# Attention's weight pieces in one transfer each instead of four, v stored from GpSimd's queue, and later loads of w_o and of attention's output

## The chip, the core and the metric

The kernel runs on one NeuronCore of a Trainium2 chip. Its five engines work at the same time and wait for each other through semaphores: TensorE (PE, with its weight loads as PEld), VectorE (DVE), ScalarE (ACT), GpSimd (POOL) and SyncE (SP), which here only issues DMA transfers. Sixteen DMA engines move data between the chip's memory (HBM) and the on-chip memory (SBUF, 128 partitions). The metric is device time in microseconds (us).

## The reference

One layer for x of 2048 rows by 448, in float32: attention with 16 heads of 28 columns, and a gated feed-forward network of width 1792, mixed row by row with a sigmoid gate.

```python
def _A_ref(x, wqkv, wo):
    qkv = transpose((x @ wqkv).reshape(B, S, 3, H, Dh), 2, 0, 3, 1, 4)
    q, k, v = qkv[0], qkv[1], qkv[2]
    scores = einsum("bhqd,bhkd->bhqk", q, k) * (Dh ** -0.5)
    p = softmax(scores, axis=-1)
    o = einsum("bhqk,bhkd->bhqd", p, v)
    return transpose(o, 0, 2, 1, 3).reshape(B, S, D) @ wo

def _B_ref(x, w_gate, w_up, w_down):
    return (gelu(x @ w_gate) * (x @ w_up)) @ w_down

g = sigmoid((x * gate_w).sum(-1, keepdims=True))
return g * _A_ref(x, wqkv, wo) + (1 - g) * _B_ref(x, w_gate, w_up, w_down)
```

## The kernel before

A float32 product is made of three products of rounded parts (high times high, high times low, low times high), so most operands exist as a high and a low half, which `parts` makes with a copy and a subtraction.

The program has four stages, one after the other on PE.

1. **q and k** (to about 82 us). `qk_tile` makes 28 tiles of q and k, which SP stores to `qkd`. On the side, x is loaded a second time in another layout (`xraw`, `load_x32`, 32 rows for each of four groups of partitions) and split by DVE into `X32`. Four groups of 32 partitions let four small matrix products run at the same time on PE, one for each quarter of the rows of x.
2. **v** (to about 116 us). `v_tile` makes 16 tiles of v. After every fourth, a group of four (928 KB) is stored to `vd`, from ACT's queue. Two buffers `V` are used in turn, so ACT may write the third group only when the store of the first has landed. At the same time `prepare(b)` splits a block of w_up or w_gate on GpSimd and stores it to `wsd` in an order of its own: per block two half-steps of 32 rows. `load_piece(m)` reads one piece of it back, into a tile `w0` (1024 columns) or `w1` (768 columns), once into each of the four groups of partitions, because each group needs the same weights for its own quarter of x. Each tile has three buffers.
3. **Attention** (about 117 to 819 us). PE interleaves three kinds of products: the scores of a head (`b<-Q,K`), the feed-forward network's x @ w_up and x @ w_gate (`b<-X,w`, called crosses), and after each half head the weights times v (`b<-pt,VH`). The order of all of it is made before the kernel runs by `plan`, which counts time with fixed costs: each of the four groups walks through its crosses in steps (`pos[r]`, starting at `OFFSET` and ending at `goal[r]`), 21 steps to two pieces, and a `load` stands where the group that is furthest back has left an old piece behind. ACT takes the exponentials, DVE copies finished crosses to `u`, SP stores them to `ud`. `finish` and `divide` send the row sums of a head through memory (`dend`, `r`, `rdend`, `rb`) on GpSimd's queue, and store the head's output to `od`.
4. **Down** (about 835 us to the end). The last block's crosses (`PG`, the last four pieces, 112 to 115) stand at its beginning, from 819 us. Then 56 units (`UNITS`, four blocks of 512 rows times `NF` = 14) each load `hu` and `hg` from `ud`, apply gelu, multiply, split into `hl`, and PE multiplies by w_down (`b<-W,hl`, 12 products to a unit). `load_wo` loads and splits w_o, `load_o` a quarter of attention's output, `project` multiplies them, and `gather` scales the results by the gate and adds them.

What sets the order of the DMA transfers: SP's queue is issued strictly in the program's order, and one transfer that waits holds up all behind it. Besides waits on data, each transfer on SP and ACT counts on one of eight semaphores that are used in turn, and waits until the transfer before it on the same semaphore has landed; GpSimd's queue has eight of its own.

Of the kernel before, what the change touches and what calls it, by code (L numbers as in the profile page):

```python
# [7 lines left out]
F32 = mybir.dt.float32  # L8
# [8 lines left out]
S, D, H, DH, F = 2048, 448, 16, 28, 1792  # L17
P = 128
# [5 lines left out]
NF = F // P  # L24
# [20 lines left out]
NEVER = 1 << 60  # L45
# [6 lines left out]
def piece(n):  # L52

    return n // 21 * 2 + (n % 21 >= 12)


def plan(blocks):
# [5 lines left out]
    goal = [21 * blocks + o for o in OFFSET]  # L63
    pos = list(OFFSET)
# [9 lines left out]
    def take():  # L74
        b = bank.index(min(bank))
        bank[b] = NEVER
        return b
# [23 lines left out]
    def run_dve(ready):  # L101
        nonlocal dve
        dve = max(dve, ready) + COPY
        return dve + BACK
# [17 lines left out]
    def can_cross(r):  # L122
        return pos[r] < goal[r] and piece(pos[r]) < parted

    def step():
        nonlocal now, parted, loaded
        did = []
        for r in range(4):
            if score[r]:
                key, b, n = score[r]  # L130
                ops.append(("score", r, key, n, b))
                score[r][2] += 1
                did.append((r, True))
            elif can_cross(r) and (mine[r] or min(bank) <= now):
                first = mine[r] is None
                mine[r] = ["cross", r, pos[r], take() if first else mine[r][3], first, False]
                ops.append(mine[r])
                pos[r] += 1
                did.append((r, False))
        now += STEP  # L140
        for r, s in did:
            if s and score[r][2] == 3:
                end_score(r)
            if not s and (pos[r] % 42 == 0 or pos[r] == goal[r]):
                mine[r][-1] = True
                b, mine[r] = mine[r][3], None
                bank[b] = run_dve(now + SEEN)
                ops.append(("clear", r, pos[r] - 1, b))
        while loaded < 2 * blocks + 8 and piece(min(pos)) >= loaded - 5:
            ops.append(("load", loaded))  # L150
            loaded += 1
            arrive.append(now + LOAD)
        while arrive and arrive[0] <= now:
            arrive.pop(0)
            parted += 1
# [59 lines left out]
def gated_mix(ctx: ExitStack, tc: tile.TileContext, xT, wqk, wvg, wg, wu, wd, wo, sel, ident, out):  # L215
    nc = tc.nc

    pin = tc.keep_in_program_order

    def mm(o, lhsT, rhs, start, stop):  # L220
        return pin(nc.tensor.matmul(o, lhsT, rhs, start=start, stop=stop))  # L221

    def by_sp(out, in_):
        return pin(nc.sync.dma_start(out=out, in_=in_))  # L224

    def by_pool(out, in_):
        return pin(nc.gpsimd.dma_start(out=out, in_=in_))  # L227
# [5 lines left out]
    def act_copy(o, i):  # L233
        return nc.scalar.activation(o, i, AF.Copy)  # L234
# [6 lines left out]
    vd = dram.tile([P, 4, H, 4, VC], F32, name="vd")  # L241
    wsd = dram.tile([2 * NF, 2, 32, 14, P], F32, name="wsd")
    shd = dram.tile([H, 2, S], F32, name="shd")
    od = dram.tile([D, S], F32, name="od")
    dend = dram.tile([H, S], F32, name="dend")
    rdend = dram.tile([H, S], F32, name="rdend")
# [9 lines left out]
    def group(r):  # L256
        return slice(32 * r, 32 * r + 32)
# [6 lines left out]
    def load_x32():  # L264
        c, k, n = UNITS[len(xraw)]
        j, b = (c, k) if k < 4 else (2 + c, k - 4)
        raw = st.tile([P, 2, TB], F32, name="xraw", bufs=2)
        for r in range(4):
            by_sp(raw[group(r), 0:n], xT[r, 32 * j:32 * j + 32, b:b + n])
        xraw.append(raw)  # L270

    def split_x32(u):
# [22 lines left out]
    def load_piece(m):  # L295
        c, a = divmod(m, 2)
        b = c // 2 if c < WRAP else len(BLOCKS) - 1 if c >= WRAP + 2 else 0
        w = halves[m] = fw.tile([P, 2, 4 - a, P], F32R, name=f"w{a}", bufs=3)
        for r in range(4):
            by_sp(w[group(r)].bitcast(F32), wsd[b, c % 2, :, 8 * a:8 + 6 * a].rearrange("p (a n) m -> p a n m", a=2))  # L300

    def step_of(n):

# [21 lines left out]
        parts(Qt[h % 2][:, 0], Qt[h % 2][:, 1], qraw, pool_copy, pool_sub)  # L325

    def load_shift(h, dma):
        for r in range(4):
            half = slice(r // 2 * 1024, (r // 2 + 1) * 1024)
            dma(Qt[h % 2][32 * r + DH:32 * r + DH + 2, 0].bitcast(F32), shd[h, :, half])  # L330

    with ExitStack() as ph:
        xp = ph.enter_context(tc.tile_pool(name="xp", bufs=1, side="right"))
# [135 lines left out]
        Qt = [p.tile([P, 2, S // 2], F32R, name=f"Q{j}") for j, p in enumerate((kt, kq))]  # L469
# [8 lines left out]
        def v_tile(i):  # L478
            V = VS[i // 4 % 2]
            p = psv.tile([P, VW], F32, name="pv")  # L480
            for j, (x, w) in enumerate(PAIRS):
                m = mm(p, X[:, x, i * P:(i + 1) * P], WV[:, w, :], j == 0, j == len(PAIRS) - 1)
            a = pin(act_copy(V[:, :, i % 4, 0:DH], p[:, 0:D].rearrange("p (h d) -> p h d", h=H)))
            pin(act_copy(gate[:, 0, i:i + 1], p[:, D:D + 1]))
            if i % 4 == 3:
                pin(nc.scalar.dma_start(out=vd[:, i // 4], in_=V))
            return m, a

        prepare(0)
# [7 lines left out]
        for m in range(2):  # L497
            load_piece(m)
# [35 lines left out]
    with tc.If(bounded < 1, label="rows"):  # L534
        with ExitStack() as ph:
# [5 lines left out]
            for h in range(H):  # L541
                Q = gp.tile([DH, 2, S], F32R, name="gQ")
                K = gp.tile([DH, 2, S], F32R, name="gK")
                for first, dst in ((h * DH, Q), (D + h * DH, K)):
                    raw = gp.tile([DH, S], F32, name="graw")
# [3 lines left out]
                m = gp.tile([P, NT], F32, name="gm")  # L549
                for i in range(NT):  # L550
                    p = gps.tile([P, S], F32, name="gsc")
                    for c in range(S // 512):
                        for n, (a, b) in enumerate(((0, 0), (1, 0), (0, 1))):
# [11 lines left out]
                                  in_=ms.bitcast(F32))  # L565
# [7 lines left out]
    ends, sums = [], {}  # L573

    def finish(h, o):
        for j in range(4):
            by_pool(dend[h:h + 1, j * 512:(j + 1) * 512], o[j * 32 + DH:j * 32 + DH + 1])
        r = op.tile([P, S // P], F32, name="r")
        by_pool(r, dend[h].rearrange("(p n) -> p n", p=P))
        ends.append((h, o, r))  # L580

    def divide():
        while ends:
            h, o, r = ends.pop()
            pin(nc.vector.reciprocal(r, r))
            by_pool(rdend[h].rearrange("(p n) -> p n", p=P), r)
            rb = op.tile([P, 512], F32, name="rb", bufs=1)
            for j in range(4):
                by_pool(rb[j * 32:(j + 1) * 32], rdend[h:h + 1, j * 512:(j + 1) * 512].to_broadcast([32, 512]))
            pin(nc.gpsimd.tensor_tensor(o, o, rb, OP.mult))  # L590
            for j in range(4):
                by_pool(od[h * DH:(h + 1) * DH, j * 512:(j + 1) * 512], o[j * 32:j * 32 + DH])
# [171 lines left out]
    def gather(tb, p, g, i):  # L764

        t = tb * 4 + i
        w = gate[:, g, t:t + 1]
        if t in Y:
            y = Y.pop(t)
            pin(nc.vector.scalar_tensor_tensor(y, p[:, 0:D], w, y, OP.mult, OP.add))  # L770
            outs.append((out[0, t * P:(t + 1) * P], y))
        else:
            y = Y[t] = yp.tile([P, D], F32, name="y", bufs=8)
            pin(nc.vector.tensor_scalar(y, p[:, 0:D], w, None, OP.mult))
# [14 lines left out]
    def load_o(tb):  # L789
        s = slice(tb * TB, (tb + 1) * TB)  # L790
        o = wl.tile([P, 4, TB], F32, name="oraw", bufs=2)
        by_pool(o[:, 0:3], od[0:3 * P, s].rearrange("(b p) n -> p b n", p=P))
        for a in (0, 64):
            by_pool(o[a:a + 64, 3], od[3 * P:, s])
        O = OHL[tb] = wl.tile([P, 7, TB], F32R, name="ohl", bufs=2)
        hr = wl.tile([P, TB], F32R, name="ohr")
        parts(O[:, 0:3], O[:, 4:7], o[:, 0:3], pool_copy, pool_sub)
        pin(pool_copy(O[0:64, 3], o[0:64, 3]))
        parts(hr[64:], O[64:, 3], o[64:, 3], pool_copy, pool_sub)

    pd, OHL = [None] * 4, {}
    for n in range(4):
        load_unit(n)
    for n in range(3):
# [7 lines left out]
    for k in range(42):  # L812
        w, a, i, j = step_of(42 * len(BLOCKS) + k)
# [9 lines left out]
    for n, (tb, f) in enumerate(UNITS):  # L823
        while outs:
            by_sp(*outs.pop(0))
        if n + EARLY < NF:
            split_f(n + EARLY)
        if n + 4 < len(UNITS):
            load_unit(n + 4)
        if n + 3 < len(UNITS):  # L830
            multiply(n + 3)
        if n + 2 < len(UNITS):
            split_unit(n + 2)
        if n in (2, 4, 6, 8):
            last_gate(n // 2 - 1)
        if n == 2:
            divide()
        if n == 3:
            load_wo()
        if n in (8, 20, 30, 44):  # L840
            load_o((8, 20, 30, 44).index(n))
        if f == 0 and tb > 1:
            for a in range(tb - 2 if tb == 2 else 1, tb):
                if a < tb - 1 or tb == 3:
                    project(a)
        down(n)
        if f == NF - 1:
            for i in range(4):
                gather(tb, pd[i], 2, i)
    project(NTB - 1)  # L850
    while outs:
        by_sp(*outs.pop(0))
# [37 lines left out]
```

## Time and profile before

| | us |
|---|---|
| three runs | 1020.56, 1024.32, 1024.58 (median 1024.32) |
| the profiled execution | 1018.83 |
| its span, from the first instruction to the last | 1017.0 |
| PE busy in the span | 994.0 (98%) |
| ACT, DVE, POOL busy | 647.3, 564.1, 481.1 |
| DMA | 194.87 MB, mean 192 GB/s |

The profile shows one execution. "Busy" is the time in which an engine has an instruction; for PE the ends of pipelined products are modelled. A row of the view by stretches (`A:B`) gives for each engine the busy time and the number of instructions, then the granted clock of PE, the mean busy share of the 16 DMA engines and the GB/s that they moved. A timeline row gives the start, the time, the engine, the line, the operation and in brackets the idle time before it with what ended it. `x4` is the number of instructions that a row merges. SPq and ACTq are the DMA-issuing sequencers of SP and ACT. In the list of DMA queues, q1 is SP's.

### The profile page before, as it was taken

How to read it: one execution, taken by the hardware profiler on the slowest of the kernel's cores; microseconds unless marked ns; L12 is line 12 of the kernel's file. 1: busy time of each engine (PE TensorE's matmuls, PEld its weight loads, DVE VectorE, ACT ScalarE, POOL GpSimd, SP SyncE). 2: the span in 40 equal slices, each digit the busy share in tenths (PEclk: the TensorE clock that was granted, in tenths of full speed). 3: DMA queues.
4: the chain of work that ended last, by engine and by line, in shares of the span. 5: the costliest groups of instructions: out<-in, count | busy, mean ns of one | idle time of the engine just before them, and what ended most of it. 6: DMA issues, size and time to landing. Idle time of an engine off the chain costs nothing.

```text
span 1017.0 us, 27987 instructions
## 1 busy us (share of the span) xinstructions
PE 994.0 (98%) x11191; PEld 754.8 (74%) x11191; DVE 564.1 (55%) x851; ACT 647.3 (64%) x1238; POOL 481.1 (47%) x697
## 2 busy tenths in 40 slices
PE   9999799989999999999999999999999999999998
PEld 7888666757766777667767667776777668899997
DVE  4552055646655676546646456664666547776552
ACT  4332176868786788867878768887787845443230
POOL 5325251735566465653556657474554204534110
PEclk9999989999999999999999999999999999999999
DMA  6866665556666666655576566665657679868350
GB/s 228 252 207 209 209 211 171 172 155 174 190 187 172 182 183 189 199 158 172 156 207 195 151 201 183 196 194 163 176 176 226 190 236 305 254 200 282 112 203 36
DMA packets 109671, 194.87 MB, mean 192 GB/s; under 512 B 32736, under 2 KB 47200, under 8 KB 109536
## 3 DMA queue, kind: packets, MB, share of 16 engines
q1 hardware_dynamic: 92272, 162.12, 51.9%
q0 software_dynamic: 15856, 26.32, 9.3%
q10 hardware_dynamic: 1408, 4.59, 1.2%
q8 instruction: 90, 1.47, 0.6%
q14 instruction: 45, 0.37, 0.1%
HBM read 131.99 MB, written 60.95 MB: 190 GB/s over the span
## 4 chain that ended last, share of the span: by engine, by line
PE 79%; DMA 5%; DVE 2%; SPq 1%; issue 0%; ACT 0%; ACTq 0%; DVEq 0%
PE b L221 79%; DMA w<-wsd 3%; DMA draw<-in_wd 1%; DMA hg<-ud 1%; SPq L224 1%; DVE hu L746 1%; DVE hl L231 0%; DVE W L231 0%; ACT hg L734 0%; DMA Q<-shd 0%; DVE u L635 0%; DVE u L633 0%; DVE o L651 0%; DVE y L770 0%; ACT W L234 0%
## 5 line engine op out<-in xcount | busy, mean ns | idle before, releaser
L221 PE MATMUL b<-X,w 32*128 32x512 f32 x4704 | 480.0, 394 | 12.5 <-DMA w<-wsd 12.2
L221 PE MATMUL b<-Q,K 32*128 32x512 f32 x3072 | 445.3, 397 | 1.8 <-DMA Q<-shd 1.7
L221 PEld LDWEIGHTS b<-X,w 32*128 32x128 f32 x4704 | 413.9, 185 | 38.5 <-issue 14.8
L618 ACT ACTIVATE pt<-b 128x512 f32<-128x512 f32 x559 | 310.1, 604 | 163.6 <-PE b L221 158.2
L221 PEld LDWEIGHTS b<-Q,K 32*128 32x128 f32 x3072 | 356.2, 183 | 34.7 <-issue 19.9
L622 DVE COPY pt<-b 128x512 f32<-128x512 f32 x465 | 312.7, 689 | 72.6 <-PE b L221 52.2
L618 ACT ACTIVATE pt<-pt 128x512 f32<-128x512 f32 x465 | 268.3, 632 | 0.1
L221 PE MATMUL b<-pt,VH 128*32 128x512 f32 x2048 | 228.1, 597 | 0.0
L221 PEld LDWEIGHTS b<-pt,VH 128*32 128x32 f32 x2048 | 63.8, 110 | 146.4 <-issue 139.2
L221 PE MATMUL b<-W,hl 128*128 128x448 f32 x672 | 139.5, 369 | 3.0 <-DVE hl L231 3.0
L221 PEld LDWEIGHTS b<-W,hl 128*128 128x128 f32 x672 | 127.1, 190 | 15.0 <-DVE hl L231 4.2
L635 DVE COPY u<-b 128x512 f32<-128x512 f32 x108 | 73.0, 684 | 34.1 <-PE b L221 33.4
L221 PE MATMUL pqk<-X,WQK 128*128 128x512 f32 x308 | 74.2, 403 | 0.3 <-ACT X L234 0.3
L734 ACT ACTIVATE hg<-hg 128x512 f32<-128x512 f32 x52 | 32.6, 626 | 65.2 <-DMA hg<-ud 64.6
L653 DVE TENSOR_TENSOR o<-b,o 128x512 f32<-128x512 f32 x16 | 11.1, 692 | 113.4 <-PE b L221 113.4
L221 PEld LDWEIGHTS pqk<-X,WQK 128*128 128x128 f32 x308 | 59.3, 193 | 15.5 <-ACT X L234 1.0
L651 DVE COPY o<-b 128x512 f32<-128x512 f32 x16 | 11.1, 691 | 106.6 <-PE b L221 86.4
L227 POOL DMA_DIRECT2D wsd<-whl x112 | 59.2, 535 | 11.0 <-POOL whl L231 8.2
L746 DVE TENSOR_TENSOR hu<-hg,hu 128x512 f32<-128x512 f32 x52 | 45.2, 869 | 30.1 <-ACT hg L734 29.9
L227 POOL DMA_DIRECT2D dend<-o x64 | 31.1, 492 | 49.9 <-DVE o L653 43.1
L227 POOL DMA_DIRECT2D rb<-rdend x64 | 31.6, 501 | 44.1 <-DMA rdend<-r 44.1
L234 ACT ACTIVATE hl<-hu 128x512 fp32r<-128x512 f32 x56 | 34.9, 623 | 25.7 <-DVE hu L746 20.9
(81 smaller groups left out, 696.5 us busy)
## 6 DMA issues: line engine op xcount, KB each, us to landing
w<-wsd SPq DMA_DIRECT2D x232, 128.0 KB
ud<-u SPq DMA_DIRECT2D x111, 256.0 KB
w<-wsd SPq DMA_DIRECT2D x232, 96.0 KB
hu<-ud SPq DMA_DIRECT2D x56, 256.0 KB
hg<-ud SPq DMA_DIRECT2D x52, 256.0 KB
qkd<-q SPq DMA_DIRECT2D x28, 256.0 KB
qraw<-qkd SPq DMA_DIRECT2D x64, 112.0 KB
kraw<-qkd SPq DMA_DIRECT2D x128, 56.0 KB
```

Source lines behind the costliest of these rows:

```text
L221: return pin(nc.tensor.matmul(o, lhsT, rhs, start=start, stop=stop))
L224: return pin(nc.sync.dma_start(out=out, in_=in_))
L227: return pin(nc.gpsimd.dma_start(out=out, in_=in_))
L234: return nc.scalar.activation(o, i, AF.Copy)
L618: pin(nc.scalar.activation(PT[key], PT[key] if b is None else sc[b], AF.Exp, scale=SCALE))
L622: pin(nc.vector.tensor_copy(PT[key], sc[b]))
L635: pin(nc.vector.tensor_copy(u, ps[b]))
L651: pin(nc.vector.tensor_copy(sums["o"], po))
L653: pin(nc.vector.tensor_tensor(sums["o"], po, sums["o"], OP.add))
L734: pin(nc.scalar.activation(o, i, AF.Gelu_apprx_tanh))
L746: pin(nc.vector.tensor_tensor(u, g, u, OP.mult))
```

## The change

Attention's weight pieces, the second copy of x (`xraw`), the shift of the scores (`Q<-shd`), the row sums (`dend`) and their inverses (`rb`) each come in one or two transfers instead of four: the four copies of a piece are written as one pattern whose reading side starts with four repeats (step 0) of 32 rows, and whose writing side is 128 partitions. A group of v is stored from GpSimd's queue instead of ACT's. The planner, when it looks for the group that is furthest back, leaves out groups that have reached their goal. w_o is loaded in unit 14 instead of 3, attention's first two quarters in units 17 and 24 instead of 8 and 20, and the four `gather`s after unit 13 are spread over units 13 to 16.

```diff
@@ plan @@
-        while loaded < 2 * blocks + 8 and piece(min(pos)) >= loaded - 5:
+        while loaded < 2 * blocks + 8 and piece(min(pos[r] if pos[r] < goal[r] else NEVER for r in range(4))) >= loaded - 5:
             ops.append(("load", loaded))
@@ load_x32 @@
         raw = st.tile([P, 2, TB], F32, name="xraw", bufs=2)
-        for r in range(4):
-            by_sp(raw[group(r), 0:n], xT[r, 32 * j:32 * j + 32, b:b + n])
+        by_sp(raw[:, 0:n], xT[:, 32 * j:32 * j + 32, b:b + n])
@@ load_piece @@
-        for r in range(4):
-            by_sp(w[group(r)].bitcast(F32), wsd[b, c % 2, :, 8 * a:8 + 6 * a].rearrange("p (a n) m -> p a n m", a=2))
+        src = wsd[b, c % 2, :, 8 * a:8 + 6 * a].rearrange("p n m -> p (n m)")
+        by_sp(w.bitcast(F32).rearrange("p a n m -> p (a n m)"),
+              src.unsqueeze(0).to_broadcast([4, 32, (8 - 2 * a) * P]))
@@ load_shift @@
-        for r in range(4):
-            half = slice(r // 2 * 1024, (r // 2 + 1) * 1024)
-            dma(Qt[h % 2][32 * r + DH:32 * r + DH + 2, 0].bitcast(F32), shd[h, :, half])
+        for a in range(2):
+            dma(Qt[h % 2][DH + a::32, 0].bitcast(F32),
+                shd[h, a].rearrange("(i n) -> i n", i=2).unsqueeze(1).to_broadcast([2, 2, S // 2]))
@@ v_tile @@
             if i % 4 == 3:
-                pin(nc.scalar.dma_start(out=vd[:, i // 4], in_=V))
+                by_pool(vd[:, i // 4], V)
@@ finish @@
-        for j in range(4):
-            by_pool(dend[h:h + 1, j * 512:(j + 1) * 512], o[j * 32 + DH:j * 32 + DH + 1])
+        by_pool(dend[h].rearrange("(j n) -> j n", j=4), o[DH::32])
@@ divide @@
-            for j in range(4):
-                by_pool(rb[j * 32:(j + 1) * 32], rdend[h:h + 1, j * 512:(j + 1) * 512].to_broadcast([32, 512]))
+            by_pool(rb, rdend[h].rearrange("(j n) -> j n", j=4).unsqueeze(1).to_broadcast([4, 32, 512]))
@@ the loop over units @@
-    pd, OHL = [None] * 4, {}
+    pd, due, OHL = [None] * 4, [], {}
-        if n == 3:
+        if n == NF:
             load_wo()
-        if n in (8, 20, 30, 44):
-            load_o((8, 20, 30, 44).index(n))
+        if n in (17, 24, 30, 44):
+            load_o((17, 24, 30, 44).index(n))
         if f == NF - 1:
-            for i in range(4):
-                gather(tb, pd[i], 2, i)
+            due = [(tb, pd[i], 2, i) for i in range(4)]
+        for _ in range(1 if NF - 1 <= n < NF + 3 else len(due)):
+            gather(*due.pop(0))
```

PE's order of instructions is the same, product by product. SP's order changes at three kinds of places.

First, on SP during the v tiles, the first six pieces (names with a number are buffers; `32x1024 x4` are four transfers of 32 rows of 1024 numbers, `128x1x1024` one transfer of 128). Before:

```order
L224 DMA wraw<-in_wu 128x512
L224 DMA w_833<-wsd 32x1024 x4
L224 DMA w_838<-wsd 32x768 x4
L224 DMA w_901<-wsd 32x1024 x4
L224 DMA w_906<-wsd 32x768 x4
L224 DMA kraw<-qkd 28x2x256 x4
```

and now:

```order
L224 DMA wraw<-in_wu 128x512
L224 DMA w_809<-wsd 128x1x1024
L224 DMA w_811<-wsd 128x1x768
L224 DMA w_871<-wsd 128x1x1024
L224 DMA w_873<-wsd 128x1x768
L224 DMA kraw<-qkd 28x2x256 x4
```

The sixteen transfers ahead of `kraw` are four, with the same bytes; the same holds for every later piece.

Second, on GpSimd at the same time, where `prepare(1)`, the split of k and `prepare(2)` follow each other. Before there is no `vd` on this queue. Now (from the split of the first k to the branch after the v tiles):

```order
L230 CAST K_704<-kraw 128x256
L231 TENSOR_TENSOR K_704<-kraw,K_704 128x256
L230 CAST K_705<-kraw 128x256
L231 TENSOR_TENSOR K_705<-kraw,K_705 128x256
L227 DMA vd<-V_714 128x1856
L230 CAST whl<-wraw 128x512
L231 TENSOR_TENSOR whl<-wraw,whl 128x512
```

The first group's store stands behind the first split. A little later on the same queue, from the end of the second split:

```order
L231 TENSOR_TENSOR K_707<-kraw,K_707 128x256
L230 CAST whl<-wraw 128x512
L231 TENSOR_TENSOR whl<-wraw,whl 128x512
L227 DMA wsd<-whl 32x1024
L227 DMA wsd<-whl 32x2x384
L227 DMA wsd<-whl 32x1024
L227 DMA wsd<-whl 32x2x384
L227 DMA vd<-V_715 128x1856
L227 DMA vd<-V_714 128x1856
L227 DMA vd<-V_715 128x1856
L533 TENSOR_LOAD flag
```

The second group's store stands behind the second split of k and all of `prepare(2)`; before, it was issued by ACT right after its last copy.

Third, on SP at the end of attention, the last pieces. Before:

```order
L224 DMA ud<-u 128x512
L224 DMA hu<-ud 128x512
L224 DMA hg<-ud 128x512
L224 DMA hu<-ud 128x512
L224 DMA hg<-ud 128x512
L224 DMA ud<-u 128x512 x2
L224 DMA w_19190<-wsd 32x1024 x4
L224 DMA w_19195<-wsd 32x768 x4
```

and now:

```order
L224 DMA ud<-u 128x512
L224 DMA w_18636<-wsd 128x1x1024
L224 DMA hu<-ud 128x512
L224 DMA hg<-ud 128x512
L224 DMA hu<-ud 128x512
L224 DMA hg<-ud 128x512
L224 DMA ud<-u 128x512 x2
L224 DMA w_18701<-wsd 128x1x768
L224 DMA w_18703<-wsd 128x1x1024
L224 DMA w_18705<-wsd 128x1x768
```

The planner now reaches pieces 114 and 115 itself (`w_18636`, `w_18701`), and the two `load_piece` calls after its loop, which are unchanged, load the same two again (`w_18703`, `w_18705`); the last crosses read the second copies.

## The prediction

> **What bounds the kernel now.** I read the table of engines first, then the chain of waits, then the costliest groups, and then the stretches of the program one by one.
>
> ```profile
> PE 994.0 (98%) x11191; PEld 754.8 (74%) x11191; DVE 564.1 (55%) x851; ACT 647.3 (64%) x1238; POOL 481.1 (47%) x697
> PE 79%; DMA 5%; DVE 2%; SPq 1%; issue 0%; ACT 0%; ACTq 0%; DVEq 0%
> PE b L221 <- DMA w<-wsd: 12.2, 7, 4.4
> PE b L221 <- DVE hl L231: 3.0, 2, 2.3
> PE b L221 <- DMA Q<-shd: 1.7, 1, 1.7
> ```
>
> PE is busy for 994.0 of 1017.0 us and makes 79% of the chain, so at most 23 us are idle. The last three rows (waited for: us, times, longest) name 16.9 of them, and each is a wait that the change touches. Since PE's own work and its order stay the same, removing all three is the most that the change can win. What it can lose is not bounded by PE at all: the other resource is the DMA engines.
>
> ```profile
> 131.50:819.00 687.50, 681.15 (x9558) 481.41 (x9550) 400.22 (x621) 532.85 (x1024) 374.98 (x586) 1.00 0.62 182
> PE b L221 <- DMA w<-wsd: 6.3, 5, 2.8
> ```
>
> This is attention (second row: PE's waits in this stretch alone). PE works 681.15 of 687.50 us at the full granted clock, while the sixteen DMA engines are busy 0.62 of the time and move 182 GB/s. There is room, but only as long as the bytes lie evenly on all sixteen.
>
> **The pieces of the weights.** The bytes stay, so the first question is how many engines carry one transfer.
>
> ```profile
> q1 hardware_dynamic: 92272, 162.12, 51.9%
> w<-wsd SPq DMA_DIRECT2D x232, 128.0 KB
> w<-wsd SPq DMA_DIRECT2D x232, 96.0 KB
> qraw<-qkd SPq DMA_DIRECT2D x64, 112.0 KB
> kraw<-qkd SPq DMA_DIRECT2D x128, 56.0 KB
> xraw<-in_xT SPq DMA_DIRECT2D x24, 128.0 KB
> xraw<-in_xT SPq DMA_DIRECT2D x8, 64.0 KB
> Q<-shd SPq DMA_DIRECT2D x4, 8.0 KB
> ```
>
> The first row counts all packets of SP's queue. SP issues 1042 transfers: the list's 496 of 32 rows (w, xraw), 192 of 28 rows (qraw, kraw), 4 of 2 rows (Q), and 350 of 128 rows. By their shapes they make 76,040 packets of data, so 16,232 of the 92,272 are something else, and in the trace these are four bytes each. That number is exactly 846 x 16 + 192 x 14 + 4 x 2: each transfer ends with one mark on each engine that it used. So 128 or 32 rows go to 16 engines, 28 rows to 14, 2 rows to 2. An engine takes an equal share of the outer rows; where 16 doesn't divide them, engines are left out.
>
> The new transfer writes 128 rows, but its reading side is 4 repeats of 32 rows, with 4 outermost. No transfer of SP before has sides that differ so that it matters. The bounds are 16 engines (the writing side decides) and 4 (a share must be equal on both sides). I take 4: the 28 and the 2 rows show that equal shares come before more engines, and a part of the new pattern that is equal on both sides is one repeat.
>
> [...]
>
> Now the price. Pieces 6 to 113 are loaded in attention: 54 x 512 KiB and 54 x 384 KiB are 49.55 MB. At present a busy engine moves 182 / (16 x 0.62) = 18.35 GB/s. A sixteenth of the pieces, 3.10 MB, is 169 us of an engine's time; its busy time is 0.62 x 687.5 = 426 us, so the other transfers take 257 us. With four engines, each of these carries 12.39 MB of pieces besides the same 257 us. How fast can one go?
>
> ```profile
> 652.80:654.70 1.90, 1.90 (x37) 1.80 (x35) 1.86 (x3) 1.84 (x5) 0.48 (x2) 1.00 0.73 214
> 676.10:676.50 0.40, 0.40 (x14) 0.40 (x10) 0.40 (x1) 0.40 (x2) 0.11 (x1) 1.00 0.95 369
> 850.00:860.00 10.00, 10.00 (x51) 9.08 (x50) 8.22 (x11) 7.49 (x14) 5.01 (x8) 1.00 0.97 320
> ```
>
> The first stretch moves pieces alone: 214 / (16 x 0.73) = 18.3 GB/s for an engine. The second is the best I found: 24.3. The third, the densest long one: 20.6. That gives three lengths of attention: at 18.35, 675 + 257 = 932 us (+245); at 24.3, 510 + 194 = 704 us, the others sped up alike (+17); at 20.6, 601 + 257 = 858 us (**+171**). I take 20.6: four engines that never rest resemble the dense stretch most, where long packets run back to back, and fewer engines at work crowd each other less than in the first row.
>
> The wait that this adds is SP's. A piece takes one engine 6.4 us (131,072 bytes at 20.6) or 4.8 us (98,304), where three buffers of each size and eight transfers in flight are the slack. Behind a w that waits for its buffer or its semaphore stand kraw, qraw and the stores of u in SP's strict order, and behind these the scores, DVE's copies and PE. A backlog that grows by a quarter of the stage's length can't be hidden by any lead, so PE waits for it in full.
>
> **The start of attention.**
>
> ```profile
> SPq L224 <- DMA vd<-V: 17.8, 3, 6.9
> 89.09 19.08 SPq L224 DMA_DIRECT2D w<-wsd  x16
> 114.55 0.40 POOL L230 CAST K<-kraw 128x256 fp32r<-128x256 f32 x1 [14.42 <-DMA kraw<-qkd]
> 119.14 2.09 POOL L227 DMA_DIRECT2D wsd<-whl  x4 [0.29 <-POOL whl L231]
> 109.70 0.54 ACT L234 ACTIVATE V<-pv 128x448 f32<-128x448 f32 x1 [1.64 <-PE pv L221]
> 124.37 2.04 PE L221 MATMUL b<-X,w 32*128 32x512 f32 x13 [4.39 <-DMA w<-wsd]
> 128.13 0.76 PE L221 MATMUL b<-Q,K 32*128 32x512 f32 x1 [1.72 <-DMA Q<-shd]
> 100.00:150.00 50.00, 43.21 (x436) 34.91 (x438) 14.11 (x21) 22.63 (x50) 18.91 (x30) 0.90 0.73 225
> ```
>
> Today SP waits 17.8 us on ACT's stores of v through the shared semaphores, and the sixteen w transfers take 19.08 us of issuing. That makes kraw late for GpSimd (14.42 us) and w and the shift late for PE (4.39 and 1.72). With the store off these semaphores, PE's 6.1 us go, and some 2 more by the clock, which stood at 0.90 over these 50 us: -8. Against it, the store of v's second group, which ACT issued at once, now stands on GpSimd behind the second split of k and `prepare(2)`. Those wait for kraw, and kraw stands behind four pieces that need 2 x 6.4 + 2 x 4.8 = 22 us from about 90. So GpSimd gets there near the 119.14 of today, and ACT, which today writes the fourth group from 109.70 into the same buffer, waits about 10 us with PE behind it: +10. Ends -8 and +15 (the store itself slow among the pieces); I take **+2**.
>
> **The second copy of x.**
>
> ```profile
> 25.00:75.00 50.00, 50.00 (x216) 40.52 (x216) 27.03 (x34) 17.98 (x32) 14.90 (x12) 1.00 0.76 231
> 40.04 0.69 DVE L230 CAST X<-xraw 128x1024 fp32r<-128x1024 f32 x1 [0.17 <-DMA xraw<-in_xT]
> ```
>
> The eight xraw transfers read four quarters of x, so the outermost count is 4 here too: 3.67 MB on four engines at 20.6 is 44.5 us. Of the 38 us that an engine is busy now (0.76 x 50), xraw's sixteenth is 12.5 at 18.35, so 26 us of others remain: 70 us into 50. DVE, whose splits are already just in time (0.17 us), then waits with q's and k's work in order behind it. q and k themselves need little of this early, and the splits have until attention, so I take **+5**, between 0 and the full +20.
>
> **The end of attention, and w_o.**
>
> ```profile
> 822.28 5.02 SPq L224 DMA_DIRECT2D w<-wsd  x8
> 827.41 7.98 PE L221 MATMUL b<-X,w 32*128 32x512 f32 x84 [1.49 <-DMA w<-wsd]
> 860.63 4.35 POOL L231 TENSOR_TENSOR WO<-oraw,WO 128x1792 fp32r<-128x1792 f32 x1
> 861.03 4.50 DVE L746 TENSOR_TENSOR hu<-hg,hu 128x512 f32<-128x512 f32 x1
> 861.16 2.74 PE L221 MATMUL b<-W,hl 128*128 128x448 f32 x12 [0.69 <-DVE hl L231]
> 866.19 40.10 PE L221 MATMUL b<-W,hl 128*128 128x448 f32 x188 [2.29 <-DVE hl L231]
> ```
>
> The last crosses read the second copies of pieces 114 and 115, and three transfers (4.8 + 6.4 + 4.8 = 16 us) start once SP is past the stores of u at 822.28. Before, the eight small ones took some 5 us and PE waited 1.49. So the end comes 6 to 10 us later: +8. On the other side, GpSimd's subtraction of w_o (4.35 us) lies beside a DVE product that takes 4.50 us, where its neighbours take 0.68, and PE then waits 2.29 + 0.69 us. In unit 14, where PE has settled at 40.10 / 188 x 12 = 2.56 us a unit and splits run two units ahead, the same 3.8 us are covered: -3. Net **+5**; 0 if the pieces arrive as before.
>
> **Priced at nothing:** SP issues 348 w transfers less, at 5.02 / 8 = 0.63 us each, but SPq has 1% of the chain. GpSimd issues fewer dend, rb and Q, off the path. The planner's line changes only the last two pieces. The moved load_o and the spread gathers lie beside PE's products; uncovered, the gathers would cost a few us at three block ends.
>
> **Sum:** 1018.83 (the profiled execution, 0.5% under the median of 1024.32) + 171 + 2 + 5 + 5 = 1202, called **1200**.
>
> **Rivals.** *Sixteen engines after all.* If the writing side's 128 rows set the number, only the gains are left: -8 at the start, -6.3 for attention's waits on w, -3 at w_o: 1018.83 - 17 = **1001**. For it: rows of 128 always go to 16 here. Against: the equal shares.
>
> *Four engines that keep up.* At 24.3 GB/s throughout, +17 less the start's 8: about **1027**, which is no change against the median. Against it: that rate is seen for 0.4 us only.
>
> *Four engines that collide.* Engines would write the four groups of partitions in step, and two of them may halve each other: 24.3 / 2 = 12.1 GB/s, 1024 + 257 = 1281 us, +594, about **1620**. For it: the stretch with pieces alone is slower (18.3) than mixed ones. Against: in the dense stretch 16 engines reach 20.6 each. [...]
>
> **How the numbers follow.** Forecast 0.77; sixteen engines 0.12; four that keep up 0.03; colliding 0.08. The forecast's own span is 1048 (at 24.3, with the small terms) to 1276 (at 18.35); I add the case that pieces are held up by each other as far as 15.5 GB/s, 799 + 257 = 1056 us, +369, with the small terms 1400. The range 1020 to 1400 takes in the forecast and the four that keep up, and leaves out 0.20. About 0.5% is what a measurement of this kernel can tell from no change: faster 0.12, same 0.03, slower 0.85.
>
> **What would show it.** SP's queue: with 118 w and 8 xraw transfers on four engines, 76,296 packets of data (two pieces are loaded twice) and 350 x 16 + 192 x 14 + 2 x 2 + 126 x 4 = 8,796 marks make 85,092; on sixteen, 86,604. In attention: PE's waits on DMA w rise from 6.3 to well over 100 us and the mean DMA share falls below 0.62. At the start: SP's 17.8 us on vd are gone, and ACT's copies of the fourth group wait on vd. At the end: no DVE product of 4.50 us near the start of the down stage. The forecast is wrong if PE hardly waits for w in attention: then the engines are sixteen, or the rate is far above 20.6.

## The result, and the profile after

The changed kernel takes 1198.57 us (median of 4 runs, 1192.55 to 1199.36), the kernel before on the same chip 1022.44: a ratio of 1.171, 95% interval 1.166 to 1.176. The forecast was 1200 with a range of 1020 to 1400. The total agrees; the next table, made from PE's first and last products of each kind in the two traces, shows that its terms agree less well.

| stretch | before, us | after, us | difference | forecast |
|---|---|---|---|---|
| q and k, to the last `pqk` | 79.4 | 82.3 | +2.9 | +5 |
| v, to the last `pv` | 37.1 | 59.0 | +21.9 | +2, with the next row |
| from there to the first score | 11.7 | 4.0 | -7.7 | |
| attention, first score to last weights times v | 691.0 | 832.4 | +141.4 | +171 |
| end of attention, to the first product with w_down | 16.2 | 38.1 | +21.9 | +8 |
| down | 168.9 | 168.9 | 0 | -3 |

From the page of the changed kernel, the engines, the chain by engine, and SP's queue and its weight pieces:

```profile
PE 1044.6 (87%) x11191; PEld 770.9 (64%) x11191; DVE 565.6 (47%) x851; ACT 654.1 (55%) x1238; POOL 426.4 (36%) x575
PE 57%; DMA 29%; SPq 1%; DVE 1%; issue 0%; ACT 0%; DVEq 0%
q1 hardware_dynamic: 85092, 163.01, 41.4%
w<-wsd SPq DMA_DIRECT2D x59, 512.0 KB
w<-wsd SPq DMA_DIRECT2D x59, 384.0 KB
```

DMA's share of the chain went from 5% to 29%. SP's queue has 85,092 packets, to the packet the number forecast for four engines (86,604 for sixteen). 8,796 of them are of four bytes in the trace, as forecast with 4 marks for each of the 118 w transfers and the 8 of xraw.

PE's waits in the whole changed kernel, and below the dots its wait for w in attention alone (145.3 to 977.7 us); the stretch row of that time follows:

```profile
PE b L221 <- DMA w<-wsd: 121.2, 33, 17.9
PE pv L221 <- ACT gate L234: 18.6, 2, 17.2
PE pqk L221 <- DVE mx L410: 3.2, 3, 1.4
...
PE b L221 <- DMA w<-wsd: 99.5, 30, 9.8
```

```profile
145.30:977.70 832.40, 732.02 (x9589) 499.08 (x9582) 402.13 (x623) 540.60 (x1025) 319.59 (x465) 0.93 0.48 149
```

PE now waits for w in attention in 30 places (before: 6.3 us in 5). The mean share of the DMA engines fell from 0.62 to 0.48 while the stage is DMA-bound: a mean over sixteen engines hides four that hardly rest. That can be worked out from the times of the packets. The w packets of attention (6731 of 4096 bytes, 6784 of 3072; q's rows, also 4096 bytes, taken off by their number) took 2310 us by the trace, 577 us on each of four engines. All the other packets took 4083 us, 255 on each of sixteen if they lie evenly. 577 + 255 = 832 us, and attention lasts 832.4. The sum can't be as exact as that: some 2% of the packets' time lies above four at once (below).

### The profile page after: what moved, and what is told of

It is laid out like the page before. It is cut to its first block, busy times and chain, and to the rows that moved or that the text cites. A ratio compares the mean times of both kernels' runs of the same rounds, so it can differ in the third digit from the quotient of the medians.

```text
span 1197.6 us, 27386 instructions
## 1 busy us (share of the span) xinstructions
PE 1044.6 (87%) x11191; PEld 770.9 (64%) x11191; DVE 565.6 (47%) x851; ACT 654.1 (55%) x1238; POOL 426.4 (36%) x575
## 3 DMA queue, kind: packets, MB, share of 16 engines
q1 hardware_dynamic: 85092, 163.01, 41.4%
## 4 chain that ended last, share of the span: by engine, by line
PE 57%; DMA 29%; SPq 1%; DVE 1%; issue 0%; ACT 0%; DVEq 0%
PE b L221 57%; DMA w<-wsd 25%; DMA hg<-ud 3%; SPq L224 1%; DMA draw<-in_wd 1%; DVE W L231 0%; DVE hl L231 0%; ACT hg L732 0%; DVE hu L744 0%; ACT W L234 0%; DVE pt L620 0%; DVE y L768 0%; DVEq L744 0%; DVEq L620 0%
## 5 line engine op out<-in xcount | busy, mean ns | idle before, releaser
L221 PE MATMUL b<-X,w 32*128 32x512 f32 x4704 | 516.7, 414 | 121.5 <-DMA w<-wsd 121.2
L221 PEld LDWEIGHTS b<-X,w 32*128 32x128 f32 x4704 | 425.6, 196 | 166.9 <-DMA w<-wsd 113.0
L221 PE MATMUL b<-Q,K 32*128 32x512 f32 x3072 | 475.1, 413 | 0.8 <-DVE pt L620 0.8
L221 PEld LDWEIGHTS b<-Q,K 32*128 32x128 f32 x3072 | 369.9, 193 | 35.4 <-issue 17.0
L221 PE MATMUL b<-pt,VH 128*32 128x512 f32 x2048 | 237.7, 618 | 0.0
L651 DVE TENSOR_TENSOR o<-b,o 128x512 f32<-128x512 f32 x16 | 11.1, 692 | 127.1 <-PE b L221 127.1
L649 DVE COPY o<-b 128x512 f32<-128x512 f32 x16 | 11.1, 692 | 123.8 <-PE b L221 114.8
L588 POOL TENSOR_TENSOR o<-o,rb 128x512 f32<-128x512 f32 x16 | 20.5, 1279 | 135.0 <-DMA rb<-rdend 135.0
L230 POOL CAST whl<-wraw 128x512 fp32r<-128x512 f32 x28 | 17.2, 615 | 117.8 <-DMA wraw<-in_wu 72.4
L221 PE MATMUL pv<-WV,X 128*128 128x450 f32 x176 | 39.8, 388 | 18.6 <-ACT gate L234 18.6
```

Of the source, the lines that this page charges most:

```text
L230: pin(copy(hi, src))
L649: pin(nc.vector.tensor_copy(sums["o"], po))
L651: pin(nc.vector.tensor_tensor(sums["o"], po, sums["o"], OP.add))
```

## Experiments

The theory: a piece in one transfer is carried by four engines, and attention is as long as these four need; v's second store costs separately because of its place on GpSimd's queue. The rivals differ from run to run.

**Undo the pieces alone (w_four).** The changed kernel with

```diff
-        by_sp(w.bitcast(F32).rearrange("p a n m -> p (a n m)"),
-              src.unsqueeze(0).to_broadcast([4, 32, (8 - 2 * a) * P]))
+        for r in range(4):
+            by_sp(w[group(r)].bitcast(F32), wsd[b, c % 2, :, 8 * a:8 + 6 * a].rearrange("p (a n) m -> p a n m", a=2))
```

> The changed kernel, with each piece of w in four transfers of 32 rows again; everything else of the change stays. Theory (one transfer of a piece uses four DMA engines, and these four are busy all through attention): attention and its end go back to the length they had before, some 150 us less than the changed kernel; what is left of the change is GpSimd's late stores of v (up to +10), so 1015 to 1040 us. SP's queue then has 76,296 packets of data and, with x still on four engines, 350 x 16 + 192 x 14 + 2 x 2 + 8 x 4 marks and 472 w transfers of 32 rows with 16 each, 15,876 in all, so 92,172. Rival (another part of the change, or the lower granted clock by itself, makes most of the loss): it stays above 1100 us.

1024.25 us, ratio to before 0.9991 (0.9966 to 1.0017). Attention takes 687.7 us and its end 18.8. The stretch row of its attention, and SP's queue:

```profile
139.20:826.80 687.60, 680.61 (x9587) 483.87 (x9579) 401.38 (x623) 533.63 (x1025) 321.15 (x465) 1.00 0.64 183
q1 hardware_dynamic: 92172, 163.04, 52.8%
```

The count is again exact. Nearly the whole loss belongs to the form of the pieces; the v tiles, at 48.7 us, don't go back, and q and k take 86.5 with x still on four engines. The first score, 4.0 us after v, and a slightly shorter attention take back a part. The profiled execution, 1028.38 us, is one of the slower of ten, and its stages add up to 9 us over the profile of before, while the medians agree.

**Do the pieces alone (w_one).** The kernel before, with the edit above reversed.

> The kernel before, with only the pieces of w in one transfer each. Theory: the loss of attention comes by itself, +134 to +145 us there, and +6 to +15 at its end, where two pieces instead of three stand in line: 1160 to 1185 us. Rival (the loss needs v's store or the later loads as well): under 1100 us.

1184.26 us, ratio 1.157 (1.152 to 1.162): attention 830.9 (+139.9), its end 28.1 (+11.9). So the form of the pieces is enough. One part was not expected: the v tiles took 47.0 us although v's store was on ACT's queue. The stretch row of attention, and ACT's timeline in w_one:

```profile
135.70:966.60 830.90, 729.22 (x9582) 492.53 (x9582) 401.18 (x622) 539.84 (x1025) 375.12 (x586) 0.94 0.48 151
...
106.24 0.56 ACT L234 ACTIVATE V<-pv 128x448 f32<-128x448 f32 x1 [1.64 <-PE pv L221]
117.34 0.33 ACTq L487 DMA_DIRECT2D vd<-V  x1
117.77 0.54 ACT L234 ACTIVATE V<-pv 128x448 f32<-128x448 f32 x1 [10.92 <-DMA w<-wsd]
```

ACT's third store is ready at 106.8 and is issued at 117.34, and what ends the wait is a landing of w. The trace has the semaphores: the store counts on the same one as the fourth of SP's w transfers here, which was issued at 98.51 and whose last landing is at 117.27. ACT's next copy stands behind the store.

**Change the number of engines (w_halves).** The kernel before, with

```diff
-        for r in range(4):
-            by_sp(w[group(r)].bitcast(F32), wsd[b, c % 2, :, 8 * a:8 + 6 * a].rearrange("p (a n) m -> p a n m", a=2))
+        src = wsd[b, c % 2, :, 8 * a:8 + 6 * a].rearrange("p n m -> p (n m)")
+        for r in range(2):
+            by_sp(w[64 * r:64 * r + 64].bitcast(F32).rearrange("p a n m -> p (a n m)"),
+                  src.unsqueeze(0).to_broadcast([2, 32, (8 - 2 * a) * P]))
```

> The kernel before, with each piece in two transfers that read 32 rows two times each. Same bytes. Theory (engines are dealt by the outermost count that both sides share, here 2, and always the same ones): all pieces lie on two engines; 49.2 MB at 20.9 GB/s an engine are 1176 us, with 254 of other work 1430 us of attention in place of 702, so about 1780 us, 1650 to 1900, with 2 marks for each of 232 transfers on SP's queue. Rival 1 (each transfer gets engines of its own, or the loss is the latency of one long transfer): the two halves run beside each other and it is no slower than with one transfer, 1180 us or less. Rival 2 (sixteen engines, slow because the same rows are read again and again): as with one transfer, about 1170 us.

1635.13 us in one run. The stretch row of its attention, and SP's queue:

```profile
160.10:1402.80 1242.70, 833.33 (x9582) 540.16 (x9582) 405.05 (x622) 549.00 (x1025) 373.46 (x586) 0.80 0.31 100
```

```profile
q1 hardware_dynamic: 85312, 162.10, 29.3%
```

232 transfers with 2 marks each give 76,040 + 9,272 = 85,312, as counted. Two transfers at once were much slower than one with the same bytes (1184.26 us in w_one), so they did not get engines of their own here, and reading rows again is not the cost: both rivals fall. The time missed the forecast's 1650 to 1900 on the low side. The pieces took 1059 us on each of two engines, 23.0 GB/s in place of the 20.9 that I had carried over from four; with 251 of other work that makes 1310 us, 5% more than the 1242.7 that attention lasted. Some 2% of the packets' time lies above two at once (below); where the rest is isn't settled.

**v back to ACT's queue (v_act).** The changed kernel with `pin(nc.scalar.dma_start(out=vd[:, i // 4], in_=V))`.

> The changed kernel, with v stored from ACT's queue again; the pieces stay in one transfer. Theory (ACT waits for the late second store of v, 17.2 us of PE): the v tiles take 37 us again in place of 59, the waits of SP on v's store and of PE on w or the shift at the start of attention come back with some 5 to 10, so 10 to 17 us less than the changed kernel, 1181 to 1190 us. Rival (the four engines are behind from the start, and the time that v loses is time in which they catch up): the same as the changed kernel within 4 us.

1189.64 us, ratio to before 1.160 (1.155 to 1.164; the changed kernel had 1.166 to 1.176). v takes 48.1 us in place of 59.0, not the 37 expected: ACT's store waits 11.48 us for a landing of w, as in w_one. The first score comes 11.5 us after v again. The whole is 8 us shorter between the two profiles and some 12 by the ratios, at the lower end of the 10 to 17 that were expected, because ACT's queue suffers from the four engines as well.

**v's second store first (v_first).** The changed kernel with

```diff
                 load_k(0, 2)
+            if i == 7:
                 split_k(0, 2)
-            if i == 6:
                 prepare(2)
```

> The changed kernel, with v's second store ahead of the second split of k and of prepare(2) on GpSimd's queue; the loads of pieces 4 and 5 move behind it too. Theory (the v tiles lose 22 us only because this store is queued behind work that waits for kraw): ACT's wait of 20.3 us on the store goes, the v tiles take 38 to 45 us in place of 59 (the first store stays where it is), and the first scores come some 5 to 10 us later after them than now, since kraw and the pieces are then what is late: in all 8 to 18 us less, 1180 to 1190 us. Rival (the four engines hold up the store itself): v stays above 52 us.

1187.96 us (2 runs), ratio 1.161 (1.155 to 1.167). The v tiles take 38.4 us, so the store's place behind the late kraw was what held PE there. The next wait took much of it back. In v_first's timeline of SP and PE after v:

```profile
97.27 13.86 SPq L224 DMA_DIRECT2D kraw<-qkd  x4
...
131.48 1.78 SPq L224 DMA_DIRECT2D Q<-shd  x2
...
137.00 0.76 PE L221 MATMUL b<-Q,K 32*128 32x512 f32 x1 [8.80 <-DMA Q<-shd]
```

The four kraw transfers, behind pieces on four engines, take 13.86 us to be issued (3.70 in the kernel before), what follows them on SP is late too, and the first score comes 16.6 us after v, not the 9 to 14 expected.

**No second loads (no_double).** The changed kernel without

```diff
-        for m in range(2):
-            load_piece(2 * WRAP + 6 + m)
```

> The changed kernel without the second loads of the last two pieces: PE's last crosses read the copies that the planner's own loads bring. Theory (the 38 us between the last weights times v and the first product with w_down are a queue of transfers on four engines, and the second copies of 114 and 115 are the last in it): PE's wait of 17.9 us falls to 2 to 8, the stretch to 24 to 29 us, the whole to 1184 to 1190 us. Rival (the stretch is long because SP issues late behind the stores of u, whatever w does): it stays within 4 us of 38.

1184.46 us (2 runs), ratio 1.158 (1.153 to 1.163). The end of attention falls from 38.1 to 29.0 us, as w_one's 28.1 had suggested: the second copies are 9 us of it, the rest is the queue on four engines that remains. PE's 17.9 us became waits of 3.25 and 4.09.

**x alone (x_one).** The kernel before with `by_sp(raw[:, 0:n], xT[:, 32 * j:32 * j + 32, b:b + n])`.

> The kernel before, with only the second copy of x in one transfer a piece. Theory (four engines carry it, DVE's splits come late, and DVE's maxima for q and k stand behind them in order): the q and k stage takes 3 to 8 us longer, nothing else changes: 1022 to 1032 us. Rival (it is early enough to be hidden): the stage takes 79.4 us within 1.

1028.11 us, ratio 1.0047 (1.0024 to 1.0069). q and k take 82.7 us (+3.3), and PE waits 3.6 us for DVE's maxima, which stand behind the splits. The whole is 5 us slower. In the profile, the down stage is 4.8 us longer as well, but its length also varies between kernels that don't touch it (below).

**All that is left (best).** The changed kernel with w and x in four transfers each, no second loads, and the order of v_first.

> The changed kernel with w and x in four transfers each, no second loads, and v's second store ahead of the second split of k. Theory (the parts that do not share engines are worth something: v off the semaphores of SP and ACT, the later loads of w_o): q and k 79 us, v 37 to 40, 5 to 8 us to the first scores, attention 685 to 690, its end 14 to 17, down 166 to 169: 8 to 14 us less than before, 1009 to 1016 us. Rival (each gain is taken back by the next wait): within 4 us of before.

1005.66 us, ratio 0.985 (0.981 to 0.988): faster than both kernels, and below the forecast. Its engines and the granted clock in slices, by the page, and PE's waits:

```profile
PE 983.5 (98%) x11191; PEld 748.0 (75%) x11191; DVE 559.9 (56%) x851; ACT 647.2 (65%) x1238; POOL 427.9 (43%) x575
PEclk9999999999999999999999999999999999999999
```

```profile
PE b L221 <- DVE pt L620: 3.7, 2, 2.7
PE b L221 <- DMA w<-wsd: 3.7, 4, 1.9
PE warm L221 <- DVE zero L351: 1.5, 1, 1.5
```

The first score comes 5.0 us after v, attention takes 687.9, its end 11.5, down 167.8. PE's wait for w fell from 12.2 to 3.7 us, and the clock has no slice under 0.9.

**Its parts (v_only, planner, wo_early).** The kernel before with v's stores on GpSimd's queue in the order of v_first; the kernel before with the planner's line and without the needless loads; and best with these lines put back:

```diff
-        if n == NF:
+        if n == 3:
             load_wo()
-        if n in (17, 24, 30, 44):
+        if n in (8, 20, 30, 44):
...
-        for _ in range(1 if NF - 1 <= n < NF + 3 else len(due)):
+        for _ in range(len(due)):
```

> The kernel before with v stored from GpSimd's queue, and v's second store ahead of the second split of k and of prepare(2). Theory (the gain of the change's first step, as it was priced: PE's 6 us at the start of attention go with SP's waits on v, while ACT has nothing to wait for): v tiles 37 us, 4 to 7 us to the first scores in place of 11.7, the whole 1014 to 1019 us beside 1023. Rival (the sixteen w transfers are issued no faster, so w stays late): 11 us or more to the first scores, and no change of the whole.

> The kernel before with the planner's new line, and without the two loads after its loop, which it makes needless. Theory (piece 114 is asked for some units of work earlier, so the last crosses don't wait): the stretch from the last weights times v to the first product with w_down takes 11 to 13 us in place of 16.2, the whole 3 to 5 us less. Rival (w comes from a queue that is busy with the stores of u anyway): 16 us still.

> The fastest kernel so far, with the loads of w_o and of attention's output and the four gathers where the kernel before has them. Theory (the later loads are worth the 3 us of PE's wait at w_o): the down stage takes 170 to 173 us in place of 168, the whole 1008 to 1011 us beside 1006. Rival (the place is worth nothing): the same within 1.5 us.

v_only: 1012.97 us, ratio 0.991 (0.988 to 0.994), 4.0 us from v to the first score in place of 11.7. planner: 1019.80 us, ratio 0.997 (0.995 to 0.9995), the end of attention at 11.5 us. wo_early: 1012.21 us, ratio 0.990 (0.988 to 0.993), down at 174.7 us where best has 167.8. The theories of the first two hold for their stages; their totals lie just outside what was expected, v_only 1 us below 1014, planner 2.8 us under before in place of 3 to 5. wo_early missed its 1008 to 1011: the later loads were worth 6 to 7 us here, more than the 3 forecast, though the two intervals touch.

The transfers of the shift and of the row sums that became fewer (`Q<-shd`, `dend`, `rb`) were never run alone, and the prediction priced those of GpSimd's queue at nothing. Attention takes 687.0 to 687.9 us in the three kernels that have them with w in four transfers (w_four, best, wo_early) and 691.0 to 692.7 in the four that have w in four transfers without them (before, x_one, v_only, planner). v's store and the planner's line alone leave it at 692.5 and 692.7, so these transfers may be worth some 4 us; it isn't shown.

## Why the prediction was right, and where its terms were not

**Four engines.** This step held to the packet, in the changed kernel, w_four and w_halves. The prediction was made without a run of unequal sides. Now there are two: a transfer with 4 x 32 rows on one side and 128 on the other left 4 marks, and one with 2 x 32 and 64 left 2. The number of marks is that of the repeats here, not that of the rows that are written. The rival of sixteen engines is out by w_four against w_one, and the rival of colliding engines, whose halving was a guess, by the rates: 20.96 GB/s on each of four engines, 23.0 on each of two, not 12.1.

The sum also lays all pieces on the same four engines (12.39 MB on each). That was assumed; no run shows which engines they are, since the trace doesn't name the engine of a packet. But it has each packet's start and time, so one can count how many are under way at once. The packets of 3072 bytes on SP's queue are all of w. In attention, the kernel before has five or more of them at once for 108 of the 156 us in which there is any; the changed kernel has four at once for 146 of 294 us and more than four for 17; w_halves has two at once for 360 of 477 us and more than two for 19. So the w transfers that are under way together rarely have more than four packets between them, and in w_halves more than two, as they would on the same four engines and the same two. The time of w_halves agrees: 1635.13 us, where 1180 or less was expected of two transfers on engines of their own. The time above the four or the two is some 2% of the packets' time. If it is packets that overlap on one engine, which the trace can't show, adding up packets overstates an engine's work by about as much.

**The price.** The forecast's 601 us of pieces on each of four engines were 577, and the other transfers took 255 in place of 257. The rate was right (20.96 against 20.6), but 1.1 MB of the pieces counted lie outside the stage. That four engines would resemble the dense stretch, and crowd each other less than sixteen, was argued, not measured: in attention, the packets of 3072 bytes went at 18.0 GB/s an engine in the kernel before and at 22.4 in the changed kernel. Of the 30 us by which attention came shorter than forecast, 14 are these bytes, 10 the rate, 2 the other transfers, and 3.5 the edges of the stage.

**How PE loses it.** The prediction says that "PE waits for it in full", with waits of "well over 100 us" as a sign. That sign was not quite met. Of the 141.4 us, 93.2 are waits for w (6.3 before, 99.5 now), and 47.4 are PE's own products in the stage, 684.6 us before and 732.0 now, at a clock of 0.99 and 0.93. The length is set by the transfers either way, so the sum didn't suffer, but "PE's own work" doesn't stay the same: over the whole kernel it is 994.0 us before, 1044.6 changed and 983.5 in best. Of the 17 us that best wins, 10.5 are shorter products and not waits that are gone.

**The start.** Here a step was mis-sized: "GpSimd gets there near the 119.14 of today", and ACT "waits about 10 us". Four rows of the changed kernel, from the timelines of GpSimd, ACT and PE, tell it:

```profile
120.60 0.40 POOL L230 CAST K<-kraw 128x256 fp32r<-128x256 f32 x1 [16.53 <-SPq L534]
...
127.19 1.14 POOL L227 DMA_DIRECT2D vd<-V  x2
...
133.20 0.54 ACT L234 ACTIVATE V<-pv 128x448 f32<-128x448 f32 x1 [20.34 <-DMA vd<-V]
133.86 7.45 PE L221 MATMUL pv<-WV,X 128*128 128x450 f32 x22 [17.20 <-ACT gate L234]
```

119.14 was the start of the four stores of wsd that stand ahead of v's, not their end (2 us more); kraw came 6 us later than before; and the store takes 6 us to land, which the sum left out. ACT is idle from 112.86, so its wait of 20.3 us is 6.3 to that 119.14, then 8 until the store is issued, and 6 of landing. The gain of 8 us was right: v_only shows 7.7. On sixteen engines the place of the store still costs 11.6 us of v (w_four), so about half of the 21.9 belongs to the order on GpSimd's queue and half to kraw, which the four engines make late.

**The end.** Mis-sized as well: "three transfers (4.8 + 6.4 + 4.8 = 16 us) start once SP is past the stores of u". SP and PE in the changed kernel:

```profile
984.00 4.49 SPq L224 DMA_DIRECT2D ud<-u  x2
988.76 6.21 SPq L224 DMA_DIRECT2D w<-wsd  x3
...
1008.41 7.49 PE L221 MATMUL b<-X,w 32*128 32x512 f32 x84 [17.91 <-DMA w<-wsd]
```

The transfers took 19.7 us from the first issue, near the forecast. But SP is past u's stores 11.1 us after the last weights times v, where it took 3.2 before. These 7.9 us, which the forecast had left out, are most of the 13.9 that it is short of; the transfers are the other 6. Of SP's delay, 3.4 us is a wait for a landing of w. The four loads of hu and hg ahead of u's stores also take 6.2 us to be issued, where they took 1.6; why isn't shown.

**x and w_o.** x cost 2.9 us, 3.3 by itself, within its bounds. The profile of before, at 79.4 us, has the longest q and k of its kind: with x in four transfers these take 77.9 to 79.4 us (7 profiles, median 78.1), with x in one 82.0 to 86.5 (6, median 82.5). So x is nearer 4.4 us, and the forecast of 5 was better than the table shows. At w_o the two waits of PE (2.29 and 0.69 us) are gone from the changed kernel, but 1.87 and 1.05 us at another place, where hg is late, took their room, so the profile shows no gain. Over all kernels the down stage takes 168.9 to 175.6 us with w_o early (7 profiles, median 174.7) and 167.8 to 176.3 with w_o late (6, median 168.5). The ranges overlap almost whole; by the medians and by wo_early the -3 was too small rather than wrong, and the profile of before that it was read from is the shortest of its kind.

The errors cancel: -29.6 in attention, +12.2 at the start, +13.9 at the end, +3 at w_o, -2.1 at x. The main term and its cause were right; that the sum came within 2 us of the result is luck. (One count in the prediction is off without effect: SP issues 346 w transfers less, 464 to 118, not 348.)

## What to carry to other kernels

Before several transfers become one, look at the outermost count of both sides of the new pattern: a repeat of 4 there brought 4 marks a transfer in place of 16 here, and alone (w_one) 139.9 us more of attention, while the mean share of the DMA engines in the profile fell from 0.62 to 0.48 and seemed to show room. Count the marks in the queue's packets, and divide the packets' time by the engines that they used, before reading a mean. When a store is moved to another queue, price the landing and the end of what stands ahead of it, not its start.

## What the runs showed that was not expected

Slow transfers on one queue held up an engine that only issues on another, through the semaphores they share: in w_one and v_act, ACT's store of v and the copies behind it waited 10.9 and 11.5 us for landings of w. And the clock was lower where PE waited more: in attention, PE waited 99.5 us for w in the changed kernel at a granted clock of 0.93, and 409.0 us in w_halves at 0.80, against 6.3 us at 0.99 in the kernel before. The same 11,191 products took 1044.6 us in the changed kernel in place of 994.0. Since 577 + 255 us of transfers already fill attention, that slower PE probably cost nothing further there; no run separates the two.
